# Two of the last matrix's 28 rows loaded by sixteen eight-partition transfers, and the last parts reordered, in a decode kernel that streams a key-value cache

## The chip, the cores and the metric

The kernel runs on one core of one Trainium2 chip. The metric is the device time of one execution in microseconds (us), as the median of repeated runs. A core has five instruction streams that matter here: TensorE (PE, matrix multiplications; its weight loads are listed as PEld), VectorE (DVE), ScalarE (ACT), GpSimd (POOL) and SyncE (SP). SP computes nothing in this kernel; it issues the transfers from the chip's memory (HBM) to the core's on-chip memory (SBUF, 128 partitions), and 16 DMA engines carry them out.

## The reference

One token of a transformer block is decoded. Its width is 1024; there are 32 query heads over 4 key-value heads with a cache of 65,536 positions, all in bf16:

```python
xn = layernorm(x)
# A: attention over the cache
q = (xn @ wq)                                  # 1024 x 4096 weights, 32 heads of 128
p = softmax(q k^T * 128**-0.5)                 # k_cache: 4 heads x 65536 x 128
A = (p v) @ wo                                 # v_cache the same size, wo 4096 x 1024
# B: an MLP block on the same xn
x1 = xn + shifted(gelu(layernorm(xn) @ w1)) @ w2
B = x1 + gelu(layernorm(x1) @ w3) @ w4         # w3 1024 x 3584, w4 3584 x 1024
out = x + A + B
```

The two caches are 64 MiB each, and with all the weights the core reads 169.87 MB once.

## The kernel before, in words

The cache is worked through in 32 steps of 8192 positions, eight to a key-value head (`for n in range(NT)`). Keys lie in `Kn` and values in `Vn`, each a tile of two slots; one transfer fills a slot, which serves two steps (its two halves). In a step, DVE transposes the next step's keys out of `Kn` into `X` (`Ttr`, L476), PE multiplies them by the prepared queries (`QK`, L488), the exponentials are taken with a running bound of the maximum, PE multiplies by the values (`PV`, L536), and POOL adds the step to the head's sum (`FLASH`).

All loads are issued by SP from one list, in the order in which the Python program makes them. Before each, SP waits until the tile to be overwritten has been read. So a load further down the list is not issued before the loads ahead of it, whatever is free. A load of rows of a weight matrix goes through the helper `load_rows` (L272): the matrix of 128 x r rows is seen as 128 partitions of r rows each, and one transfer brings a stretch of some of the r rows to every partition. Such a transfer has 128 pieces of `rows x 2 KB`, one for each partition.

The weights w1, w2, w3 and the first two quarters of wo are loaded into `W` between the steps and used some steps later. The last matrix, w4, has 28 rows in each partition. It is loaded at the end, in the parts that the table `w4_parts` lists as (first row, rows, slot of `Kn`, offset in the slot). The loop at L619 to L624 does this at step n = 30, when step 31's keys are about to be transposed. Slot 0 of `Kn` is free from step 29's transposes on; slot 1 holds step 31's keys and is free when DVE has transposed them (about 373.6 us in the profile).

After the loop PE does what is left: the last two quarters of wo (`wo_pe`), the normalization of the last head (`combine_1`, `combine_2`), and then `w4_pe(i)` for each part i in the table's order. `w4_pe` calls `out_rows`, which makes four small matrix multiplications (L404) for each row, all of them added into `OUT_ps`. Each part has a semaphore of its own (`"w4%d" % i`) and PE waits for the whole part. Then DVE copies `OUT_ps` to `orow` (L631) and SP stores it with a transfer of four rows (L632).

Of the kernel before, what the change touches and what calls it, by code (L numbers as in the profile page):

```python
# [72 lines left out]
def _deps(q, reads, writes):  # L73
    for b in reads:
        for s, v in b.w.items():
            q.wait((s, v))
    for b in writes:
        for s, v in b.w.items():
            q.wait((s, v))
        for s, v in b.r.items():  # L80
            q.wait((s, v))


def _done(ev, reads, writes, partial=False):
    for b in reads:
        b.add_read(ev)
    for b in writes:
        if partial:
            b.add_write(ev)
        else:  # L90
            b.set_write(ev)
# [24 lines left out]
def _dma(q, chan, fn, reads=(), writes=(), partial=False):  # L116
    _deps(q, reads, writes)
    chan.n += 1
    ev = q.dma(fn, chan.sem, 16 * chan.n)
    _done(ev, reads, writes, partial)  # L120
    return ev


def bass_parallel_sum__gqa_block_cached__mixer_s_mlp__decode_kernel(
# [14 lines left out]
    D = A_x.shape[2]  # L139
# [15 lines left out]
    with ExitStack() as es:  # L155
        E = es.enter_context

        def sb(name, shape, dt):
            return E(nc.sbuf_tensor(name, shape, dt))
# [4 lines left out]
        def sem(name):  # L164
            return E(nc.semaphore(name))
# [56 lines left out]
        Kn = sb("Kn", [P, 2, 16384], BF)  # L222
# [15 lines left out]
        q_sp = _Q("sp", None)  # L238
        chans = {}

        def chan(name):
            if name not in chans:
                chans[name] = _DmaChan(sem("d_" + name))
            return chans[name]
# [22 lines left out]
        def rows_src(w, r0, nrow):  # L267
            return w.rearrange("(p r) n -> p r n", p=P)[:, r0:r0 + nrow, :]

        def load_rows(dst, bufs, ch, w, r0, nrow):  # L270
            ncol = w.shape[1]
            _dma(q_sp, chan(ch), lambda e: e.dma_start(out=dst.rearrange("p (r n) -> p r n", n=ncol), in_=rows_src(w, r0, nrow)),  # L272
                 writes=bufs)
# [301 lines left out]
                 (16, lambda: wo_dma(0), 19, lambda: wo_pe(0)), (20, lambda: wo_dma(1), 23, lambda: wo_pe(1))]  # L575
        at_dma = {n: f for n, f, _, _ in w_seq}
        at_pe = {n: f for _, _, n, f in w_seq}
        w4_parts = [(0, 14, 0, 0), (14, 8, 1, 0), (22, 4, 1, 8), (26, 2, 0, 14)]

        def w4_dma(i):  # L580
            r0, nr, s, o = w4_parts[i]
            load_rows(Kn[:, s, o * D:(o + nr) * D], [b_W4[i]], "w4%d" % i, B_w4, r0, nr)

        b_W4 = [_B() for _ in w4_parts]

# [5 lines left out]
        for n in range(NT):  # L591
# [27 lines left out]
            if n == NT - 2:  # L619
                for i in range(len(w4_parts)):  # L620
                    for bk in b_K[w4_parts[i][2]]:
                        for sv, vv in bk.r.items():
                            b_W4[i].add_read((sv, vv))
                    w4_dma(i)  # L624
# [43 lines left out]
```

## Time and profile before

| | |
|---|---|
| median of 3 runs | 403.05 us (402.99 to 403.19) |
| span of the profiled execution, first to last instruction | 401.7 us |
| time outside the span, by the median | 1.4 us |
| PE, DVE, ACT, POOL busy | 46%, 57%, 12%, 15% |
| read from HBM | 169.87 MB, 423 GB/s over the span |
| landing of the last part of w4 | 398.8 us |
| last matrix multiplications end, copy to `orow` begins | 399.5 us |

The span is the profiled execution's own clock, from its first to its last instruction; times inside it are counted from its start. The run's time has some 1.4 us more. "DMA share" in a view is the mean busy share of the core's 16 DMA engines. The profile has no line for a single DMA engine, and nothing in it numbers them; how many are busy is read from the share. Every transfer ends with one completion mark from each DMA engine that took part, and the trace keeps the time of each mark.

### The profile page before, as it was taken

What the parts mean: (1) busy time and instruction counts of PE and PEld (TensorE: products, weight loads), DVE (VectorE), ACT (ScalarE), POOL (GpSimd) and SP (SyncE); (2) the same over time, 40 slices, a digit from 0 to 9 for tenths busy, and PEclk for the clock granted to TensorE, in tenths of its full rate; (3) what the DMA queues carried; (4) which work ended last, traced back from release to release, by engine and by line L of the source; (5) the groups of instructions that cost most, each with busy time, mean ns of one, the idle gap of its engine ahead of it and who ended that gap; (6) DMA issues with size and microseconds to landing.
All of it is one profiled execution on the core that took longest, in us unless ns stands there. A gap on an engine that the chain in (4) does not pass through costs nothing.

```text
span 401.7 us, 4776 instructions
## 1 busy us (share of the span) xinstructions
PE 186.4 (46%) x1859; PEld 78.5 (20%) x1875; DVE 228.4 (57%) x401; ACT 48.9 (12%) x128; POOL 61.8 (15%) x90
## 2 busy tenths in 40 slices
PE   0332325064525745285531965353433654444664
PEld 0211101021103511062110731121111311111132
DVE  0247566277816578255744287576836775788410
ACT  1000111011101011011110011111201111112100
POOL 5000003012211011110310101111110112112110
PEclk9985556556565556555655555656555656565566
DMA  8999999999999999999999999999999999999994
GB/s 359 424 418 438 445 418 424 460 419 421 436 447 419 429 435 435 422 436 445 420 428 450 426 419 441 441 419 428 434 439 421 447 432 424 426 425 436 437 416 207
DMA packets 7087, 170.19 MB, mean 424 GB/s; under 512 B 916, under 2 KB 920, under 8 KB 1048
## 3 DMA queue, kind: packets, MB, share of 16 engines
q1 hardware_dynamic: 6920, 169.87, 98.4%
q8 instruction: 15, 0.25, 0.2%
q14 instruction: 8, 0.07, 0.0%
q10 hardware_dynamic: 144, 0.00, 0.0%
HBM read 169.87 MB, written 0.00 MB: 423 GB/s over the span
## 4 chain that ended last, share of the span: by engine, by line
DMA 55%; DVE 24%; PE 16%; issue 2%; ACT 1%; SPq 0%; another core or an unknown queue 0%; POOL 0%; ACTq 0%
DMA Kn<-in_A_k_cache_dram 44%; DVE X L476 13%; DMA Kn<-in_B_w_dram 6%; DMA Vn<-in_A_wq_dram 5%; PE H_ps L366 4%; PE S_ps L488 3%; DVE pT_f L529 3%; PE OT_ps L536 3%; DVE mrow L495 3%; PE M_ps L366 1%; ACT p_sb L518 1%; PE PT_ps L527 1%; PE M_ps L564 1%; PE OUT_ps L404 1%; DVE Yall L393 1%
## 5 line engine op out<-in xcount | busy, mean ns | idle before, releaser
L476 DVE STREAM_TRANSPOSE X<-Kn 128x1024 f32<-128x1024 f32 x128 | 151.7, 1215 | 67.4 <-DMA Kn<-in_A_k_cache_dram 67.4
L536 PE MATMUL OT_ps<-Vn,pT_f 128*32 128x512 bf16 x512 | 60.7, 627 | 52.4 <-DVE pT_f L529 52.4
L488 PE MATMUL S_ps<-X,Yall 128*32 128x512 bf16 x512 | 59.1, 608 | 16.1 <-DVE X L476 16.1
L501 PE MATMUL MB_ps<-Rm,Lmat 128*128 128x16 bf16 x32 | 6.1, 192 | 90.1 <-DVE Rm L496 90.1
L550 POOL TENSOR_TENSOR O_acc<-O_acc,tmpO 128x513 f32<-128x513 f32 x28 | 32.8, 1172 | 88.6 <-ACT tmpO L544 88.6
L518 ACT ACTIVATE p_sb<-S_ps,brun 128x512 bf16<-128x512 f32 x32 | 22.0, 687 | 192.7 <-DVE brun L516 157.3
L548 POOL TENSOR_SCALAR O_acc<-O_acc,ff 128x513 f32<-128x513 f32 x28 | 19.5, 698 | 153.4 <-ACT ff L523 153.4
L495 DVE TENSOR_REDUCE mrow<-S_ps 128x1 f32<-128x512 f32 x32 | 21.6, 674 | 25.5 <-PE S_ps L488 25.5
L544 ACT ACTIVATE tmpO<-OT_ps 128x512 f32<-128x512 f32 x32 | 19.1, 598 | 108.0 <-PE OT_ps L536 108.0
L488 PEld LDWEIGHTS S_ps<-X,Yall 128*32 128x32 bf16 x512 | 16.6, 126 | 54.7 <-DVE X L476 38.2
L529 DVE STREAM_TRANSPOSE pT_f<-PT_ps 128x512 f32<-128x512 f32 x32 | 22.9, 716 | 6.1 <-PE PT_ps L527 4.2
L536 PEld LDWEIGHTS OT_ps<-Vn,pT_f 128*32 128x32 bf16 x512 | 14.6, 129 | 59.2 <-DVE pT_f L529 42.0
L501 PEld LDWEIGHTS MB_ps<-Rm,Lmat 128*128 128x128 bf16 x32 | 3.3, 102 | 114.9 <-DVE Rm L496 114.9
L527 PE MATMUL PT_ps<-p_sb,permR 128*128 128x512 bf16 x16 | 9.3, 580 | 21.4 <-ACT p_sb L518 21.4
L366 PEld LDWEIGHTS H_ps<-xn_bf,W 128*128 128x128 bf16 x224 | 14.4, 169 | 1.7 <-issue 1.7
L366 PE MATMUL H_ps<-xn_bf,W 128*128 128x1 bf16 x224 | 14.5, 202 | 0.0
L527 PEld LDWEIGHTS PT_ps<-p_sb,permR 128*128 128x128 bf16 x32 | 3.4, 105 | 41.4 <-ACT p_sb L518 41.4
L505 DVE TENSOR_REDUCE Bst<-MB_ps 128x1 f32<-128x16 f32 x32 | 5.6, 174 | 8.3 <-PE MB_ps L501 8.3
L330 PE MATMUL M_ps<-ln_s,ones_f 128*128 128x1 f32 x6 | 1.8, 362 | 17.3 <-DVE ln_s L329 17.3
L546 POOL COPY O_acc<-tmpO 128x513 f32<-128x513 f32 x4 | 2.4, 612 | 47.4 <-ACT tmpO L544 47.4
L404 PE MATMUL OUT_ps<-Kn,gh_bf 128*1 128x256 bf16 x112 | 5.6, 364 | 5.0 <-DMA Kn<-in_B_w_dram 5.0
L631 DVE CAST orow<-OUT_ps 128x256 bf16<-128x256 f32 x1 | 0.4, 425 | 12.7 <-PE OUT_ps L404 12.7
(109 smaller groups left out, 116.6 us busy)
## 6 DMA issues: line engine op xcount, KB each, us to landing
Kn<-in_A_k_cache_dram SPq DMA_DIRECT2D x15, 4096.0 KB, 27.3
Vn<-in_A_v_cache_dram SPq DMA_DIRECT2D x15, 4096.0 KB, 23.3
W<-in_B_w_dram SPq DMA_DIRECT2D x2, 3584.0 KB, 24.9
W<-in_A_wo_dram SPq DMA_DIRECT2D x3, 2048.0 KB, 23.8
Kn<-in_A_wq_dram SPq DMA_DIRECT2D x1, 4096.0 KB, 12.1
Vn<-in_A_wq_dram SPq DMA_DIRECT2D x1, 4096.0 KB, 21.2
W<-in_B_w_dram SPq DMA_DIRECT2D x2, 2048.0 KB, 33.8
Kn<-in_A_k_cache_dram SPq DMA_DIRECT2D x2, 2048.0 KB, 25.3
```

What stands on the lines that cost most here:

```text
L366: fns.append(lambda e, j=j, cx=cx: e.matmul(ps_tile[:, c0 + cx:c0 + cx + 1], lhs_fn(j - j0, cx), rhs_fn(j), start=(j == 0 and cx == 0), st ...
L404: fns.append(lambda e, lhs=lhs, rhs=rhs, jj=jj: e.matmul(OUT_ps[32 * jj:32 * jj + 1, 0:256], lhs, rhs[:, 256 * jj:256 * jj + 256], start=F ...
L476: _op(q_dve, lambda e, ix=ix: e.transpose(out=X32[:, xs, 1024 * ix:1024 * (ix + 1)], in_=Kn32[:, s, 4096 * half + 1024 * ix:4096 * half + ...
L488: fns.append(lambda e, we=we, cm=cm, mv=mv: e.matmul(S_ps[32 * cm:32 * cm + 32, :], Yall[:, h, we, :, :].rearrange("p a g -> p (a g)"), mv ...
L495: _op(q_dve, lambda e: e.reduce_max(mrow[:, m:m + 1], S_ps[:, :], axis=AX.X), reads=[b_S], writes=[b_mrow[m]])
L518: _op(q_act, lambda e: e.activation(p_sb[:, m, :], S_ps[:, :], ACTF.Exp, bias=brun[:, kn:kn + 1], scale=SCALE, accum_out=tmpO[:, m, 512:513]),
L527: _op(q_pe, lambda e: e.matmul(PT_ps[:, :], permR[:, :], p_sb[:, m, :], start=True, stop=True), reads=[b_p[m], b_const], writes=[b_PT])
L529: _op(q_dve, lambda e: e.transpose(out=pT_f[:, :], in_=PT_ps[:, :]), reads=[b_PT], writes=[b_pT])
L536: fns.append(lambda e, q=q, q4=q4: e.matmul(OT_ps[32 * q4:32 * q4 + 32, :], pT_bf[:, q, :, 1], Vn[:, s, 8192 * half + 512 * q:8192 * half ...
L544: _op(q_act, lambda e: e.activation(tmpO[:, m, 0:512], OT_ps[:, :], ACTF.Copy), reads=[b_OT], writes=[b_tmpO[m]], partial=True)
L548: _op(q_pool, lambda e: e.tensor_scalar(out=O_acc[:, :], in0=O_acc[:, :], scalar1=ff[:, m:m + 1], scalar2=0.0, op0=ALU.mult, op1=ALU.add), ...
L550: _op(q_pool, lambda e: e.tensor_tensor(out=O_acc[:, :], in0=O_acc[:, :], in1=tmpO[:, m, :], op=ALU.add), reads=[b_tmpO[m]], writes=[b_Oacc])
```

## The change

Two rows of w4 that were in the third part, rows 24 and 25, are loaded as a part of their own. It goes to slot 0, behind the first part, in place of rows 26 and 27, and is the second part in the table. It is not loaded by one transfer over 128 partitions but by sixteen transfers of eight neighbouring partitions each, with one semaphore that PE awaits at 256 (sixteen times 16). Rows 22 and 23 and rows 26 and 27 become the last two parts, in slot 1, two rows each. PE takes the parts in the new order.

```diff
-        w4_parts = [(0, 14, 0, 0), (14, 8, 1, 0), (22, 4, 1, 8), (26, 2, 0, 14)]
+        w4_parts = [(0, 14, 0, 0), (24, 2, 0, 14), (14, 8, 1, 0), (22, 2, 1, 8), (26, 2, 1, 10)]
 
         def w4_dma(i):
             r0, nr, s, o = w4_parts[i]
-            load_rows(Kn[:, s, o * D:(o + nr) * D], [b_W4[i]], "w4%d" % i, B_w4, r0, nr)
+            dst = Kn[:, s, o * D:(o + nr) * D]
+            if i == 1:
+                src = rows_src(B_w4, r0, nr).rearrange("p r n -> p (r n)")
+                for g in range(16):
+                    _dma(q_sp, chan("w41"), lambda e, g=g: e.dma_start(out=dst[8 * g:8 * g + 8, :], in_=src[8 * g:8 * g + 8, :]),
+                         writes=[b_W4[i]] if g == 0 else [], partial=False)
+                b_W4[i].set_write((chan("w41").sem, 16 * 16))
+                return
+            load_rows(dst, [b_W4[i]], "w4%d" % i, B_w4, r0, nr)
```

The bytes loaded, PE's multiplications and the work of DVE, ACT and POOL stay the same in number and size.

## The prediction

> **What bounds the kernel now.** I read the page's slices first. The DMA rows of the 40 slices say that transfers run from the start to the last slice, and no engine's row does:
>
> ```profile
> DMA  8999999999999999999999999999999999999994
> GB/s 359 424 418 438 445 418 424 460 419 421 436 447 419 429 435 435 422 436 445 420 428 450 426 419 441 441 419 428 434 439 421 447 432 424 426 425 436 437 416 207
> ```
>
> So the end is set by bytes, and an edit matters where it changes how the 16 DMA engines share the last of them. The chain of waits for the last 30 us confirms it. It runs from SP's last issue into one DMA piece, and only 2.8 us (401.66 - 398.81) come after the landing:
>
> ```profile
> 374.44 24.37 DMA Kn<-in_B_w_dram
> 398.81 0.04 issue
> 398.85 0.63 PE OUT_ps L404 x6
> ...
> 399.50 0.42 DVE orow L631
> ```
>
> Third, the busy windows of the tail (start:end length, then x = counts, with PEclk, DMA share and GB/s as the last three columns) tell how many DMA engines are still at work:
>
> ```profile
> 392.00:394.00 2.00, 1.36 (x32) 0.69 (x20) 0.00 (x0) 0.00 (x0) 0.00 (x0) 0.74 0.98 416
> ...
> 395.50:396.00 0.50, 0.50 (x28) 0.40 (x20) 0.00 (x0) 0.00 (x0) 0.00 (x0) 1.00 0.61 254
> ...
> 397.00:397.50 0.50, 0.00 (x0) 0.00 (x0) 0.00 (x0) 0.00 (x0) 0.00 (x0) 0.50 0.42 172
> 397.50:398.00 0.50, 0.37 (x8) 0.24 (x12) 0.00 (x0) 0.00 (x0) 0.00 (x0) 0.50 0.36 147
> 398.00:398.50 0.50, 0.50 (x16) 0.14 (x4) 0.00 (x0) 0.00 (x0) 0.00 (x0) 0.50 0.04 16
> ```
>
> A share of 0.42 is 6.7 engines of 16. All work until 395; then nine run dry within two microseconds, and seven go on to 398. The trace's sixteen completion marks of the last transfer say the same: eight from 395.36 to 396.68, one at 396.94, seven from 398.16 to 398.81. At the first key load all sixteen marks lay within 0.4 us. The gap grew by about 1.5 us on one engine at a time. The page's queue rows name the only other traffic that could do this:
>
> ```profile
> q1 hardware_dynamic: 6920, 169.87, 98.4%
> q8 instruction: 15, 0.25, 0.2%
> q14 instruction: 8, 0.07, 0.0%
> q10 hardware_dynamic: 144, 0.00, 0.0%
> ```
>
> Fifteen instruction blocks of 16 KB on q8, one engine each, delayed eight engines, most of them twice; the eight small packets of q14 explain the lesser delays. That is read from the times of blocks and marks, not from a row of its own. So bytes are shared equally and seven engines are late.
>
> **The change, part by part.** *How many engines one small transfer uses.* The vector x (queue q10) makes 144 packets: 128 pieces and 16 marks. On q1 there are 48 transfers of that kind, 48 x 144 = 6912, and eight packets remain for the four-row store: four pieces and four marks. Four rows thus used four engines, so eight rows will use eight. Which eight, and whether each time the same, no row shows; I take the same eight. [...]
>
> *The moved bytes.* Full share moves 416/0.98 = 424 GB/s, or 26.5 GB/s for one engine. A 4 KB piece takes 0.155 us. One 128-partition transfer of two rows gives each engine eight pieces, 1.24 us. After the change eight engines have sixteen pieces (2.48 us) and the others none. So eight engines have 1.24 us more to do and eight have 1.24 us less; the sum is unchanged.
>
> *The marks.* The eight engines make sixteen completion marks instead of one; the trace's mark packets are 0.009 us each, so fifteen more cost about 0.1 us. If the following piece is already under way it is nothing.
>
> *The pieces' own speed.* All large transfers now spread over all 128 partitions; no row shows eight engines writing eight neighbouring ones. Lower bound: as now, 0.155 us. Upper bound: a whole transfer (32 KB) at one engine's speed, 1.24 us, times 16 = 19.8 us instead of 2.5. The slices' rates (416 to 460 GB/s wherever the share is 9) show no slowing anywhere, so I stay near the lower end, and keep a doubling (2.48 us more) as the case that the range has to hold. [...]
>
> *SP's queue.* Behind part 0 (issued at 359.62, 0.43 us) stand sixteen issues, now ahead of the wait for slot 1. SP's waits have
>
> ```profile
> SPq L272 <- DVE X L476: 13.5, 1, 13.5
> ```
>
> so there is 13.5 us of cover. One issue took 0.33 to 0.43 us for the weights and 0.65 us for the four-row store: sixteen with 0.05 us gaps are 6 to 11 us. All hidden. If they overran, the parts behind would be issued later than 373.6, but part 0 lands only at 386.8 to 390.3, so the engines would still not run dry. I cost it at nothing. The new part waits for nothing new: slot 0 was awaited by part 0.
>
> *PE.* Parts 0 and 1 are taken 14 + 2 rows, then 8, 2, 2. The last part still has eight multiplications (0.59 us at a granted clock of 0.50) behind its landing; before it, rows 22 and 23 (another 0.6 us) land 1.24 us earlier and are done in time. Nothing on the path, except that a clock of 1.00 would make 0.59 about 0.3.
>
> *The sum* goes by where the seven late engines stand. Last landing before: 398.81. Engines with the double share: their time + 1.24 + 0.1. Engines without: their time - 1.24.
>
> **Forecast.** At least one of the seven late engines is among the eight. Then the last landing is about 398.81 + 1.34 = 400.15 and the end moves by +1.35 us: 403.05 + 1.35 = 404.4 (own range 403.9 to 404.8, for smaller lateness of the one engine and for the marks). For it: one suffices, and nothing in the profile separates them. Chance 0.35.
>
> **Rivals.** *Faster: the late seven are exactly in the other half.* Instruction blocks went round eight engines in turn, which would be natural for a block of eight; if it is the half that the small transfers spare, the late ones end at 398.81 - 1.24 = 397.57, and the early ones at 396.68 + 1.34 = 398.0 (396.94 gives 398.3). The last landing is 398.0 to 398.3, a gain of 0.5 to 0.8 us; with the early engines less spread in another execution and PE's last group at the higher clock up to 1.4. So 402.3 (401.7 to 402.55). It decides as soon as no late engine is among the eight. Chance 0.30, of which 0.17 lies above a gain of 0.2%.
>
> *Slower by more: neighbouring partitions slow the pieces.* At twice the piece time, with the late engines elsewhere, the early ones end at 396.8 + 1.34 + 2.48 = 400.6: +1.8, 404.85. With a late one among them 398.81 + 3.82: +3.8, 406.9. Against it: no slow stretch in the slices; for it: no stretch with such transfers. Chance 0.25.
>
> *No change: the sixteen transfers do not take the same eight engines*, but spread over all. Then each engine has its old share and 403.05 stays, within 0.3. Against: four rows showed exactly four marks, which argues for a fixed rule. Chance 0.10.
>
> **The numbers.** The forecast is the likeliest case, 404.4. The range goes from 402.2, with most of the faster rival, to 407.0, the doubled piece time with a late engine; beyond are the strongest gains and a slowing above two, together about 0.2. A measurement of this kernel can tell 0.2%, 0.8 us, from no change. Faster by that: 0.17. Within: 0.13 of the faster rival and 0.10 of no change, 0.23. Slower: 0.35 + 0.25 = 0.60.
>
> **What would show it.** Step by step in the profile after: queue q1 at 47 + 1 = 48 full transfers, 6912, plus 16 x (8 + 8) = 256 and 8 packets, 7176 (sixteen marks each would give more); SP's sixteen issues inside the 13.5 us wait; the shares of the tail. If about eight engines work on behind 398.8, the forecast or the slow pieces hold; slow pieces would show as a dip of the rate between 387 and 393, the forecast would not. If the share falls for all within half a microsecond, the late ones were spared. I am wrong if the last landing is at or before 398.3.

## The result and the profile after

| | before | after |
|---|---|---|
| median | 403.02 us (402.94 to 403.19) | 406.91 us (406.78 to 407.69) |
| span of the profiled execution | 401.7 us | 405.5 us |
| last landing of w4 | 398.81 us | 402.33 us |

The changed kernel is slower: ratio 1.0101, 95% interval 1.0086 to 1.0115, or +3.9 us where +1.35 was forecast. The time lies in the forecast's range (402.2 to 407.0), but the change is almost three times the one forecast.

The queue row of the page after has the predicted packet count, 48 x 144 + 16 x (8 + 8) + 8 = 7176, so each small transfer runs on eight engines:

```profile
q1 hardware_dynamic: 7176, 169.87, 98.0%
```

The chain of waits of the kernel after (start, length, what) no longer ends in a DMA landing followed by one PE group. It leaves DMA at 399.89, the landing of the eight-row part, and PE then works through three parts in series:

```profile
373.71 26.17 DMA Kn<-in_B_w_dram
399.89 0.04 issue
399.93 1.91 PE OUT_ps L404 x32
401.83 0.14 issue
401.97 0.62 PE OUT_ps L404 x8
402.59 0.14 issue
402.73 0.62 PE OUT_ps L404 x8
403.35 0.02 issue
403.38 0.42 DVE orow L639
```

Between the two traces the windows (stretch and length, busy time and count of PE, PEld, DVE, ACT and POOL, then PEclk, DMA share, GB/s) show where the time went. A DMA piece is counted whole in the window in which it starts, so a share can pass 1. Before:

```profile
387.00:389.00 2.00, 1.80 (x32) 0.85 (x30) 0.00 (x0) 0.00 (x0) 0.00 (x0) 0.50 0.96 414
389.00:391.00 2.00, 0.63 (x16) 0.41 (x20) 0.00 (x0) 0.00 (x0) 0.00 (x0) 0.50 1.01 434
391.00:393.00 2.00, 2.00 (x44) 1.33 (x40) 0.00 (x0) 0.00 (x0) 0.00 (x0) 0.50 0.95 406
```

After:

```profile
387.00:389.00 2.00, 1.29 (x28) 0.88 (x32) 0.53 (x2) 0.00 (x0) 0.00 (x0) 0.50 1.11 318
389.00:391.00 2.00, 0.59 (x12) 0.09 (x4) 0.00 (x0) 0.00 (x0) 0.00 (x0) 0.50 0.87 260
391.00:393.00 2.00, 1.03 (x24) 0.66 (x27) 0.00 (x0) 0.00 (x0) 0.00 (x0) 0.50 1.03 332
```

The DMA share is about the same, the rate is not: 260 GB/s with engines 87% busy, against 434; over 387 to 393 us together 303 GB/s at a share of 1.00, against 418 at 0.98. The engines were not idle or fewer; each byte took longer. The trace's packets say which: the 4 KB pieces of the small transfers took 0.159 us at first and then 0.18 to 0.26 us, the 28 KB pieces of the first part, on other engines, up to 1.68 us instead of 1.06, and the 16 KB pieces up to 0.96 instead of 0.61. The first part was complete at 391.93 instead of 390.33.

### The profile page after: what moved, and what is told of

Its sections match the earlier page's. It is cut to its first block, busy times and chain, and to the rows that moved or that the text cites. A ratio compares the mean times of both kernels' runs of the same rounds, so it can differ in the third digit from the quotient of the medians.

```text
span 405.5 us, 4793 instructions
## 1 busy us (share of the span) xinstructions
PE 189.0 (47%) x1859; PEld 79.7 (20%) x1875; DVE 228.5 (56%) x401; ACT 48.9 (12%) x128; POOL 61.9 (15%) x90
## 3 DMA queue, kind: packets, MB, share of 16 engines
q1 hardware_dynamic: 7176, 169.87, 98.0%
## 4 chain that ended last, share of the span: by engine, by line
DMA 55%; DVE 24%; PE 17%; ACT 2%; issue 2%; another core or an unknown queue 0%; POOL 0%; SPq 0%; ACTq 0%
DMA Kn<-in_A_k_cache_dram 43%; DVE X L476 12%; DMA Kn<-in_B_w_dram 6%; DMA Vn<-in_A_wq_dram 5%; PE H_ps L366 4%; DVE pT_f L529 3%; PE S_ps L488 3%; PE OT_ps L536 3%; DVE mrow L495 3%; PE OUT_ps L404 2%; ACT p_sb L518 2%; PE M_ps L366 1%; PE PT_ps L527 1%; PE M_ps L564 1%; DVE Yall L393 1%
## 5 line engine op out<-in xcount | busy, mean ns | idle before, releaser
L404 PE MATMUL OUT_ps<-Kn,gh_bf 128*1 128x256 bf16 x112 | 6.6, 402 | 7.1 <-DMA Kn<-in_B_w_dram 6.8
```

The source lines that it names most:

```text
L404: fns.append(lambda e, lhs=lhs, rhs=rhs, jj=jj: e.matmul(OUT_ps[32 * jj:32 * jj + 1, 0:256], lhs, rhs[:, 256 * jj:256 * jj + 256], start=F ...
```

## Theories

*W*: neighbouring partitions are the trouble, because the eight engines write close together. *O*, formed after the second run: a piece that an engine writes into partitions which another engine is filling is slow, and it slows others. *S*: a small transfer is slow for itself, by its marks and issues, wherever it writes. *D*: the double share of eight engines is all. *H*: the slowing is in HBM, where the rows are read. A fourth question is the forecast's own condition: are late engines among the eight? In every diff below the changed kernel is the base unless another is named.

## The experiments

**The order alone** (one 128-partition transfer for rows 24 and 25):

```diff
-            if i == 1:
+            if False:
```

> The new order of the parts is kept, but rows 24 and 25 come in one 128-partition transfer. If the sixteen small transfers are the whole cost (my theory, and every rival that blames the transfers): 403.0 +/- 0.4 us, the tail's DMA share as before. If the order of the parts costs (PE has 8 + 2 + 2 rows behind the landing of the eight-row part): 403.5 or more, with PE's last groups back to back. The changed kernel had 3.5 us later landing and 0.35 us of PE work in series; this run says whether the 0.35 needs the late landing.

Measured 403.23 us, ratio to the kernel before 1.0003 (0.9993 to 1.0013). The last landing was 398.92, and the chain ends in it and one PE group, as in the kernel before:

```profile
374.97 23.95 DMA Kn<-in_B_w_dram
398.92 0.04 issue
398.96 0.62 PE OUT_ps L404 x8
```

The order of the parts costs nothing that can be told by itself; the whole loss comes with the sixteen small transfers.

**Partitions four apart, over both halves:**

```diff
                 for g in range(16):
-                    _dma(q_sp, chan("w41"), lambda e, g=g: e.dma_start(out=dst[8 * g:8 * g + 8, :], in_=src[8 * g:8 * g + 8, :]),
+                    p0 = 32 * (g // 4) + g % 4
+                    _dma(q_sp, chan("w41"), lambda e, p0=p0: e.dma_start(out=dst[p0:p0 + 29:4, :], in_=src[p0:p0 + 29:4, :]),
```

> Same sixteen transfers, same eight pieces of 4 KB each, same bytes and marks; only each transfer's eight partitions lie four apart (0, 4, .. 28; 1, 5, .. 29; ...) instead of side by side. Theory W (pieces that several engines write into neighbouring partitions slow each other, and slow the engine that fills those partitions anyway): about half of the cost above the double share goes, 405.0 to 405.8 us, and the rate between 387 and 393 us dips less than in the changed kernel (where it fell to 250 GB/s). Theory S (a small transfer has an overhead of its own, wherever it writes): 406.9 as the changed kernel. Theory D (the double share of the eight engines alone costs): 406.9 too, since the shares are the same. [...]

Measured 407.8 us, ratio 1.0118 (1.0103 to 1.0133): worse than the changed kernel, outside what W, S and D had expected. Theory W, that neighbours are the trouble, falls in that form. The rate went lower than in the changed kernel:

```profile
389.00:391.00 2.00, 0.86 (x19) 0.27 (x8) 0.00 (x0) 0.00 (x0) 0.00 (x0) 0.50 0.89 205
```

The pieces' times said more than the total: 0.159 us while the early engines worked through the first eight transfers (partitions 0 to 63), then 0.25 to 0.33 us, with a median of 0.30, in the second eight (64 to 127), about twice as long. This is what theory O was made from.

**Sixteen partitions to a transfer, eight transfers:**

```diff
-                for g in range(16):
-                    _dma(q_sp, chan("w41"), lambda e, g=g: e.dma_start(out=dst[8 * g:8 * g + 8, :], in_=src[8 * g:8 * g + 8, :]),
+                for g in range(8):
+                    _dma(q_sp, chan("w41"), lambda e, g=g: e.dma_start(out=dst[16 * g:16 * g + 16, :], in_=src[16 * g:16 * g + 16, :]),
...
-                b_W4[i].set_write((chan("w41").sem, 16 * 16))
+                b_W4[i].set_write((chan("w41").sem, 8 * 16))
```

> Eight transfers of sixteen neighbouring partitions: pieces of 4 KB as in the changed kernel, but sixteen to a transfer, so that all engines should take part and each gets its old share (eight pieces). Theory D: 403.0 to 403.3, since nothing is unequal. Theory W: slow pieces as before or worse, now on all sixteen engines, eight each: +1 to +3, 404 to 406. Theory S: eight marks instead of sixteen and eight pieces at 0.205 instead of 0.155 us, +0.4 us, 403.4. The queue's packets should be 48 x 144 + 8 x 32 + 8 = 7176.

Measured 406.09 us, ratio 1.0078 (1.0063 to 1.0093). All sixteen engines have their old share here (the queue's 48 x 144 + 8 x 32 + 8 = 7176 packets leave sixteen marks to each of the eight transfers), and it is still 3.1 us slower, a little more than theory W expected and far from D (403.0 to 403.3) and S (403.4). Theory D falls as a sole cause. The dip is there without any inequality:

```profile
387.00:389.00 2.00, 0.91 (x14) 0.50 (x17) 0.84 (x3) 0.00 (x0) 0.00 (x0) 0.50 0.92 264
389.00:391.00 2.00, 1.37 (x28) 0.57 (x20) 0.00 (x0) 0.00 (x0) 0.00 (x0) 0.50 0.98 293
391.00:393.00 2.00, 0.59 (x12) 0.38 (x16) 0.00 (x0) 0.00 (x0) 0.00 (x0) 0.50 1.16 270
```

**Where the late engines stand** (on the kernel before):

```diff
                     w4_dma(i)
+                for k in (1, 2, 4, 8):
+                    _dma(q_sp, chan("pr%d" % k), lambda e, k=k: e.dma_start(out=Kn[0:k, 1, 12288 + 256 * k:12544 + 256 * k], in_=B_w4[0:k, 0:256]))
...
+        for k in (1, 2, 4, 8):
+            q_sp.wait((chan("pr%d" % k).sem, 16))
```

> The kernel before, with four tiny transfers of 512 B a partition behind the last part, of 1, 2, 4 and 8 partitions into a free stretch of Kn, which nothing reads. Each uses as many engines as it has partitions, behind all the other work of these engines, so its landing says how late the latest of them is. If two of the seven late engines are among the eight (my reading of the changed kernel's marks: six of the eight took their first small piece at 386.5 to 387.2, two only after 391): the eight-partition probe lands at 398.2 to 399.0 with the last part, and its eight marks show six early and two late. If the late engines are all outside the eight: it lands by 397.0. The time stays 403.0 to 403.3.

Measured 403.01 us, ratio 0.9998 (0.9987 to 1.0008). The marks of the last part, ahead of the probes, were eight from 395.37 to 396.77, one at 397.22 and seven from 398.18 to 398.90. The probe of one partition came at 395.57, that of two at 395.75 and 396.62, that of four at 395.93, 395.99, 396.80 and 399.08, that of eight at 395.77, 396.10, 396.12, 396.17, 396.97, 397.68, 398.41 and 399.26. So the eight engines hold two of the seven late ones, one of them already in the four-partition probe. Each larger probe had marks 0.17 to 0.18 us behind those of the smaller one (395.57, 395.75, 395.93, 396.10; 396.62, 396.80, 396.97; 399.08, 399.26) and new ones besides, so in this run it added engines and kept the earlier ones. The forecast's condition held; the rival "late seven exactly in the other half" could not come true.

**One half only, four apart.** The next two write one half of the partitions twice and leave the other half of rows 24 and 25 out. This is the low half; for the high half `p0` begins with 64 instead of 0:

```diff
-                    _dma(q_sp, chan("w41"), lambda e, g=g: e.dma_start(out=dst[8 * g:8 * g + 8, :], in_=src[8 * g:8 * g + 8, :]),
-                         writes=[b_W4[i]] if g == 0 else [], partial=False)
+                    p0 = 0 + 32 * (g // 4 % 2) + g % 4
+                    d = dst if g < 8 else Vn[:, 0, 8192:10240]
+                    _dma(q_sp, chan("w41"), lambda e, p0=p0, d=d: e.dma_start(out=d[p0:p0 + 29:4, :], in_=src[p0:p0 + 29:4, :]),
+                         writes={0: [b_W4[i]], 8: [b_V[0][1]]}.get(g, []), partial=False)
```

> Sixteen transfers of eight partitions four apart, all into partitions 0 to 63 (each piece of these partitions is loaded twice, the second time into a free stretch of Vn; partitions 64 to 127 of rows 24 and 25 are left out, so the sum lacks them). In the run with stride four the first eight transfers, which wrote partitions 0 to 63, had pieces of 0.159 us, and the second eight, into 64 to 127, 0.289 us. Theory O (a piece is slow where another engine is filling the same partitions, and slows that engine; the eight engines fill 0 to 63 themselves in the large transfers): all pieces near 0.16 us, no dip of the rate between 387 and 393 us, part 0 complete at 390.4 as before; what is left is the double share, +1.3, 404.3 us. Theory S (small transfers are slow after the first few, for their marks or their issue, wherever they write): the second eight are slow again, 407.8.

> The mirror of the run before: all sixteen transfers into partitions 64 to 127, four apart (partitions 0 to 63 of rows 24 and 25 left out). Theory O: all sixteen pieces at about 0.29 us or more, part 0 complete 2 to 3 us later than in the kernel before, +5.5 to +7, 408.5 to 410 us. Theory S: 407.8, as with the pieces over both halves. If the halves do not matter this run and the one before have one time.

Low half: 404.63 us, ratio 1.0044 (1.0029 to 1.0059). High half: 410.16 us, ratio 1.0183 (1.0168 to 1.0198). Transfers of the same number and size differ by 5.5 us by the partitions they write; theory S falls, and O's numbers (404.3, and 408.5 to 410) hold to 0.4 us. The windows, low half:

```profile
387.00:389.00 2.00, 1.67 (x32) 0.93 (x32) 0.17 (x1) 0.00 (x0) 0.00 (x0) 0.51 0.98 410
389.00:391.00 2.00, 0.72 (x16) 0.37 (x16) 0.00 (x0) 0.00 (x0) 0.00 (x0) 0.50 0.98 408
```

and high half:

```profile
387.00:389.00 2.00, 1.74 (x32) 0.94 (x32) 0.11 (x1) 0.00 (x0) 0.00 (x0) 0.50 0.99 211
389.00:391.00 2.00, 0.13 (x4) 0.00 (x0) 0.00 (x0) 0.00 (x0) 0.00 (x0) 0.50 1.11 236
391.00:393.00 2.00, 0.00 (x0) 0.00 (x0) 0.00 (x0) 0.00 (x0) 0.00 (x0) 0.50 0.92 209
```

No dip in the one: the 4 KB pieces of the rush all took 0.159 us, and the first part was complete at 390.44, as before. In the other the whole core runs at half its rate: small pieces 0.23 to 0.33 us, most of them about 0.30, and 28 KB pieces up to 2.19 us.

**The low half with the other half's rows as source** (as the low half, with `in_=src[64 + p0:p0 + 93:4, :]`, so rows land in wrong places):

> As the run into partitions 0 to 63, but the source in HBM is the rows of w4 that belong to partitions 64 to 127 (the sum gets rows in wrong places). Only the side that is read differs. If the slowing is where the pieces are written (theory O): 404.3 us, as the low half. If it is in HBM, where two engines read the same stretch of w4's rows (theory H): as the high half, 408.5 to 410 us.

Measured 404.58 us, ratio 1.0043 (1.0028 to 1.0058): as the low half, to 0.05 us. What was read does not matter, and theory H falls:

```profile
389.00:391.00 2.00, 1.35 (x32) 0.54 (x25) 0.00 (x0) 0.00 (x0) 0.00 (x0) 0.50 0.97 406
```

**The low half, eight neighbours to a transfer** (`p0 = 8 * (g % 8)`, `d[p0:p0 + 8, :]`, the high half left out):

> Into partitions 0 to 63 again, each part of them twice, but with eight neighbouring partitions to a transfer as in the changed kernel, so that the eight engines write close together and away from the other eight. Theory O with neighbours counted (several of the eight write into one group of four partitions): pieces of 0.2 to 0.3 us, the rate dips, 405 to 407 us. If neighbours alone do no harm: 404.3 us, as four apart. The changed kernel's pieces were 0.16 us in the first transfers and 0.19 to 0.26 us later.

Measured 407.45 us, ratio 1.0113 (1.0096 to 1.013), 2.8 us more than four apart in the same half and half a microsecond above the range that O had expected. So neighbours do harm after all, in the low half too, where the rate four apart was 408 GB/s:

```profile
389.00:391.00 2.00, 0.83 (x16) 0.25 (x8) 0.00 (x0) 0.00 (x0) 0.00 (x0) 0.50 1.00 248
```

The runs fit one sentence: four apart in partitions 0 to 63 the small pieces kept 0.159 us; with eight neighbours to a transfer the rate in the same half fell from 408 to 248 GB/s; and in partitions 64 to 127, four apart, most pieces took about 0.30 us, about twice as long. Theory O reads this as engines that meet in the same partitions, by neighbourhood within a half or by crossing into the half that the other eight engines fill. Its numbers held for the low half and the high half and were half a microsecond too low for the neighbours. But nothing in the traces numbers the engines, and no run shows which engine writes which partitions, in the large transfers or the small ones; so the meeting is the author's explanation, and what was measured is the piece times, the rates and the run times by the partitions written.

## Why the prediction was right or wrong

*Right*: the bound (the last bytes' shares among the engines), eight engines for each small transfer, a late engine among the eight, the double share's price, and SP's cover. SP issued the sixteen in 5.4 us, inside its wait:

```profile
358.57 5.43 SPq L586 DMA_DIRECT2D Kn<-in_B_w_dram  x16
373.71 1.31 SPq L272 DMA_DIRECT2D Kn<-in_B_w_dram  x3
```

The low-half run is the forecast's own case, the double share without the slow pieces: forecast 404.4, measured 404.63; its last landing moved from 398.81 to 400.24, +1.43, where the sum had 1.24 + 0.1. That the times agree to 0.2 us is in part luck: beside its own runs of the kernel before (402.95) it is 1.68 us slower, and PE added 0.3 us that the sum did not have (below).

*Wrong, the step "the pieces' own speed"*: it stayed near the lower end, 0.155 us, on the ground that no slice of the profile before showed slow pieces. No slice could: every load of the caches and the weights spread over all 128 partitions there, and the only 4 KB pieces, the 128 of the last part, all took 0.159 us. Measured in the changed kernel, the small pieces took 0.18 to 0.26 us after the first ones.

*Missing from that step*: it priced only the small pieces, not what they do to the other engines. The copy to `orow` begins 403.38 - 399.50 = 3.88 us later. By the last mark of each part, taken as one engine's, this has three terms. The first part completes 391.93 - 390.33 = 1.60 us later; this is the slowing of large pieces on engines that carry no small ones yet, and the sum had nothing for it. From there to the last landing it is 10.40 us (402.33 - 391.93) instead of 8.48 (398.81 - 390.33), +1.92: the forecast's 1.34 and about 0.6 for slow pieces. The rest, 3.88 - 1.60 - 1.92 = 0.36 us, is PE.

*Also wrong, "PE: nothing on the path"*: PE ran its last twelve rows back to back, at a granted clock of 0.50 by the windows, 1.91 + 0.62 + 0.62 us with two gaps of 0.14, which outlasted the 2.44 us from the landing of the eight rows (399.89) to that of the last part (402.33). With the order alone (403.23 us) these two landings lay just as far apart (396.49 and 398.92), but the last one still led: the clock was 1.00 when the eight rows landed there, and in the changed kernel it had fallen to 0.50 by 399. First the order alone, then the changed kernel:

```profile
395.00:397.00 2.00, 0.47 (x20) 0.42 (x24) 0.00 (x0) 0.00 (x0) 0.00 (x0) 1.00 0.61 246
```

```profile
399.00:399.50 0.50, 0.00 (x0) 0.00 (x0) 0.00 (x0) 0.00 (x0) 0.00 (x0) 0.50 0.20 66
```

The low-half run, whose eight rows landed at 397.78, ends in the same series:

```profile
397.83 1.91 PE OUT_ps L404 x26
399.73 0.14 issue
399.87 0.62 PE OUT_ps L404 x8
400.49 0.14 issue
400.63 0.62 PE OUT_ps L404 x8
401.25 0.02 issue
401.27 0.42 DVE orow L641
```

Its copy begins 1.77 us later than before (401.27 against 399.50): 1.43 for the last landing and 0.34 for PE. So PE's term comes with the double share even without slow pieces.

*The rivals*: "neighbouring partitions slow the pieces", in its leg with a late engine among the eight, said 406.9 and met the number, but by another sum: twice the piece time on the small pieces alone. In truth the small pieces took 1.1 to 1.6 times as long, the large ones of the other engines were slowed too, and PE added its part; that the number came out was luck. "No change" fell with the packet count and the probes.

No version that beats the kernel before came out. Giving bytes to the engines that a small transfer takes can help only if none of them is late; by the probes two of the eight are (marks at 398.41 and 399.26), one of them among the four of the four-partition probe (399.08).

## What to carry to other kernels

Where transfers set the end, price a small transfer by the partitions it writes, not only by its bytes: here sixteen transfers of the same size took 404.63 us into partitions 0 to 63 and 410.16 into 64 to 127, and the second slowed the whole queue, with 28 KB pieces of the first part up to 2.19 us instead of 1.06. Moving load between DMA engines needs two facts first, how many engines a shape selects and how many of them are late; a few tiny probe transfers behind the last one told both here (one mark to each partition, two late ones among eight), at no cost that could be measured (403.01 us against 402.99). And a busy share near one beside a falling GB/s is the sign to look for (here 1.00 at 303 GB/s, against 0.98 at 418): engines that are busy and slow, not idle.

## What the runs showed that was not expected

- The slowing is not confined to engines that carry small pieces. By the probes only two of the seven late engines are among the eight; still in the high-half run all seven completed the first part at 392.30 to 393.73, against 389.65 to 390.33 before. The core moved 211 GB/s, half of its 424. These two have their small pieces behind the first part, and theory O assumes that in the first part they fill partitions 0 to 63, which no small piece wrote. Why they are held up too, no run tells; it stays open.
- The small transfers four apart over both halves took SP 10.80 us to issue where neighbours took 5.43, hidden in both cases.
- The sixteen engines of the kernel before, within 0.4 us of each other at the first key load, ended 3.4 us apart. Instruction blocks fit as the cause: up to 32.2 us of the trace all marks of a load lie within 0.4 us, the first packets of the two instruction queues behind the start run from 36.55 us (8 KB) and 41.43 us (16 KB), and at the next load's marks (from 41.5) two engines are 1.2 and 1.9 us behind the first. No run moved the blocks, so the cause is read from these times and not shown.
